# Attention's opening in a fused attention and mixture-of-experts kernel: what is computed while the decay mask is fetched, and the order of small work in the loop

## The chip, the core and the metric

The kernel runs on one core of a Trainium2 chip. Five engines have queues of their own: TensorE (PE), VectorE (DVE), ScalarE (ACT), GpSimd (POOL) and SyncE (SP). Each works through its queue in order. DMAs are issued from the queues of SP, ACT and POOL. The metric is the time on the device of one execution, in microseconds; smaller is better.

## The reference

Three layers follow each other: linear attention with a decay per head in blocks, a mixture of experts that routes each token to one expert, and a second mixture in which all experts contribute. The change lies in the first layer and the routing of the second.

```python
B, H, S, D = 2, 8, 768, 64          # batch, heads, sequence, head dimension
Dmask = where(rel >= 0, lam ** rel, 0)      # rel = i - j, one mask for each head
for b in range(nb):                         # blocks of the sequence
    intra = einsum('bhic,bhjc->bhij', qb, kb) * Dmask
    intra = einsum('bhij,bhjd->bhid', intra, vb)
    inter = einsum('bhid,bhde->bhie', qb * lam_pow, kv_state)
    out[:, :, sl] = intra + inter
    kb_dec = kb * rev_pow                   # rev_pow = lam ** (block - 1 - pos)
    kv_state = lam_block * kv_state + einsum('bhsd,bhse->bhde', kb_dec, vb)
# x: 1536 tokens of 512
logits = x @ w_gate + modality_bias[modality_id]
e_idx = argmax(logits);  gate_w = softmax(logits)[e_idx]
out[mask] = gate_w[mask, None] * (relu(x[mask] @ w1[e]) @ w2[e])     # 8 experts
# then the second mixture: gates balanced over rows and columns, all 8 experts summed
```

## The kernel before

The order on every engine is the order in which the code is written; nothing is rescheduled. Attention runs over M = 12 chunks of 128 tokens of one batch entry, all eight heads at once; chunk m is block m // 2 of batch entry m % 2. The function `attention_and_routing` holds all of it.

For each chunk, `load(m, 0)` and `load(m, 1)` bring the two halves of a packed input into one of four buffers `pk`: the first half holds keys and queries transposed, the second keys and values. `scores(m)` multiplies keys and queries into banks 0 and 1 of PSUM, `masked(m)` multiplies them by `maskT` on DVE, and so frees the banks. `scaled(m)` makes on POOL the decayed keys `kd` (with `revp`) and the scaled queries `qd` (with `lamq`). `outputs(m)` adds the products of `qd` with the state `St` and of values with the masked scores in bank 2, which ACT copies to `xT`; it also makes the new state from `kd` and the values in bank 3. `decay(m)` scales the state on POOL.

The mask isn't an input. DVE builds the powers of lambda in `pw`, one row a head, ACT's queue writes them to `powd` in device memory, and SP's queue reads them back in a shifted pattern as `maskT`, and as `lamq`. `revp` is a column of the mask.

The routing follows behind. `rows(m)` multiplies `xT` by an identity and the gate weights (`gtab`), so that one product gives the tokens' rows and their logits. `gates(m)` works on two chunks: it adds the modality's bias (prepared once by `setup`), finds the largest logit, the expert (`oh`), the sum of exponentials and its reciprocal `gw`, the gate weight. `weighted(m)` copies the rows with that weight and stores them to `xs`. `place(m)` counts positions within the experts, in bank 3. In step t of the loop stand `scores(t)`, `rows(t - 2)`, `outputs(t - 1)`; in odd steps also `gates(t - 3)` and the weighted copies, in even ones `place(t - 4)`. At t = 8 `early_table` picks the largest expert so far, whose weights are then loaded, and at t = 9 `ids_out` makes the row numbers of its first tokens.

## Time and profile before

| | |
|---|---|
| median of 3 timed runs | 1303.19 us (1300.23 to 1305.47) |
| profiled execution | 1302.41 us, of which the span of the trace is 1300.6 |
| PE, busy | 1256.5 us, 97% of the span |
| DVE, ACT, POOL, busy | 686.2 (53%), 499.5 (38%), 421.2 us (32%) |
| PE, first slice of 32.5 us of the span | 5 tenths |

The page gives the busy time of each engine and cuts the span in 40 slices. A line of the timeline gives the start, the time that the instructions took together, the engine, the line of the code, what is written and read, and in brackets how long the engine stood idle before it and what released it. An engine's name with a q is its queue, which issues DMAs. The granted clock is 1.00 at 2.4 GHz and 0.50 at 1.2 GHz.

### The profile page before, as it was taken

To read this page: it belongs to the slowest core of one execution; us is meant where nothing else is said; L and a number is where in the kernel's file an instruction comes from. 1 tells how busy PE (TensorE), PEld (TensorE's weight loads), DVE (VectorE), ACT (ScalarE), POOL (GpSimd) and SP (SyncE) were. 2 spreads that over 40 slices of the span, in tenths; PEclk is the share of its full clock that TensorE was granted. 3 is DMA by queue.
4 is the path that set the end of the run, shared out by engine and by line. 5 is a ranking of instruction groups with operands and counts; after the bars stand their busy time and mean duration, and the time that the engine had idled before them with its cause. 6 is when DMAs were issued, how large, how long until landed. Compare 5 with 4: busy or idle time off the path is not lost.

```text
span 1300.6 us, 19334 instructions
## 1 busy us (share of the span) xinstructions
PE 1256.5 (97%) x7266; PEld 1144.0 (88%) x7266; DVE 686.2 (53%) x1330; ACT 499.5 (38%) x996; POOL 421.2 (32%) x405
## 2 busy tenths in 40 slices
PE   5877999989999999999999999999999999999998
PEld 4867999988999999999999999999999999999997
DVE  5567787736354454545454546354535454545453
ACT  1244555531243334433434342234434343343431
POOL 3411101023333333333333336333333333333332
PEclk9988999989999999999999999999999999999999
DMA  8653565520122212221212223122222122222211
GB/s 284 204 180 115 198 197 188 163 98 1 41 65 66 74 57 74 65 65 65 74 65 74 72 74 100 58 77 66 65 74 65 66 65 65 66 73 65 69 38 49
DMA packets 60632, 117.76 MB, mean 91 GB/s; under 512 B 7288, under 2 KB 8960, under 8 KB 60528
## 3 DMA queue, kind: packets, MB, share of 16 engines
q1 hardware_dynamic: 55744, 105.67, 25.2%
q0 software_dynamic: 2304, 7.05, 1.6%
q10 hardware_dynamic: 2480, 3.71, 0.8%
q8 instruction: 59, 0.97, 0.3%
q14 instruction: 45, 0.37, 0.1%
HBM read 110.10 MB, written 6.30 MB: 89 GB/s over the span
## 4 chain that ended last, share of the span: by engine, by line
PE 78%; DVE 1%; POOL 0%; issue 0%; POOLq 0%
PE banks L887 13%; PE banks L886 13%; PE banks L885 13%; PE banks L850 12%; PE banks L851 12%; PE banks L852 12%; PE banks L723 0%; POOL out_dram L868 0%; PE banks L729 0%; PE banks L755 0%; DVE Pm L749 0%; DVE Pm L759 0%; DVE tab L747 0%; POOLq L1022 0%; DVE tab L757 0%
## 5 line engine op out<-in xcount | busy, mean ns | idle before, releaser
L839 POOL TENSOR_TENSOR w1r<-sraw,w1r 128x1024 fp32r<-128x1024 f32 x56 | 134.5, 2402 | 574.8 <-ACT w1r L838 574.8
L887 PE MATMUL banks<-w2r,hb 128*128 128x512 f32 x750 | 294.8, 393 | 0.0
L886 PE MATMUL banks<-w2r,hb 128*128 128x512 f32 x750 | 294.1, 392 | 0.0
L885 PE MATMUL banks<-w2r,hb 128*128 128x512 f32 x750 | 291.6, 389 | 0.0
L887 PEld LDWEIGHTS banks<-w2r,hb 128*128 128x128 f32 x750 | 140.7, 188 | 29.6
L855 ACT ACTIVATE hb<-snap 128x384 fp32r<-128x384 f32 x168 | 87.8, 523 | 200.7 <-DVE snap L972 120.0
L850 PE MATMUL banks<-x2T,w1r 128*128 128x384 f32 x464 | 159.3, 343 | 3.5 <-DVEq L702 3.5
L851 PE MATMUL banks<-x2T,w1r 128*128 128x384 f32 x464 | 158.9, 343 | 0.0
L852 PE MATMUL banks<-x2T,w1r 128*128 128x384 f32 x464 | 157.7, 340 | 0.0
L886 PEld LDWEIGHTS banks<-w2r,hb 128*128 128x128 f32 x750 | 140.7, 188 | 19.3
L885 PEld LDWEIGHTS banks<-w2r,hb 128*128 128x128 f32 x750 | 140.8, 188 | 19.1
L852 PE MATMUL banks<-xt,w1r 128*128 128x384 f32 x448 | 151.1, 337 | 0.0
L850 PE MATMUL banks<-xt,w1r 128*128 128x384 f32 x448 | 150.8, 337 | 0.0
L851 PE MATMUL banks<-xt,w1r 128*128 128x384 f32 x448 | 150.8, 337 | 0.0
L856 DVE SCALAR_TENSOR_TENSOR hb<-snap,hb 128x384 fp32r<-128x384 f32 x168 | 102.7, 611 | 66.4 <-ACT hb L855 66.4
L856 DVE SCALAR_TENSOR_TENSOR hb<-banks,hb 128x384 fp32r<-128x384 f32 x88 | 49.0, 557 | 165.0 <-ACT hb L855 165.0
L855 ACT ACTIVATE hb<-banks 128x384 fp32r<-128x384 f32 x88 | 43.3, 492 | 212.5 <-PE banks L852 204.9
L281 DVE TENSOR_TENSOR w2r<-stg,w2r 128x512 fp32r<-128x512 f32 x155 | 106.7, 691 | 3.7 <-ACT w2r L280 3.3
L280 ACT ACTIVATE w2r<-stg 128x512 fp32r<-128x512 f32 x155 | 96.2, 623 | 3.8 <-DMA stg<-in_w_dram 3.8
L850 PEld LDWEIGHTS banks<-x2T,w1r 128*128 128x128 f32 x464 | 88.1, 190 | 9.3 <-ACTq L702 3.7
L851 PEld LDWEIGHTS banks<-x2T,w1r 128*128 128x128 f32 x464 | 88.2, 190 | 5.7
L851 PEld LDWEIGHTS banks<-xt,w1r 128*128 128x128 f32 x448 | 84.1, 188 | 7.3
(218 smaller groups left out, 2114.4 us busy)
## 6 DMA issues: line engine op xcount, KB each, us to landing
stg<-in_w_dram SPq DMA_DIRECT2D x349, 256.0 KB
pk<-in_pack_dram SPq DMA_DIRECT2D x24, 512.0 KB
xs<-xr ACTq DMA_DIRECT2D x12, 256.0 KB
xrow<-in_w_dram SPq DMA_DIRECT2D x3, 256.0 KB
maskT<-powd SPq DMA_DIRECT2D x2, 256.0 KB
xrow<-xs,gidx POOLq DMA_INDIRECT x21
gtab<-in_gtab_dram ACTq DMA_DIRECT2D x1, 272.0 KB
lamq<-powd SPq DMA_DIRECT2D x2, 128.0 KB
```

What stands on the lines that cost most here:

```text
L280: A.activation(out=dst[:, 0], in_=src, func=AF.Copy)
L281: eng.tensor_tensor(out=dst[:, 1], in0=src, in1=dst[:, 0].bitcast(F32), op=ALU.subtract)
L839: G.tensor_tensor(out=ws[:, 1], in0=sraw, in1=ws[:, 0].bitcast(F32), op=ALU.subtract)
L850: T.matmul(out=b, lhsT=w(0, kk), rhs=x(0, kk), start=start and kk == 0, stop=False, skip_group_check=True)
L851: T.matmul(out=b, lhsT=w(0, kk), rhs=x(1, kk), start=False, stop=False, skip_group_check=True)
L852: T.matmul(out=b, lhsT=w(1, kk), rhs=x(0, kk), start=False, stop=stop and kk == kks - 1, skip_group_check=True)
L855: A.activation(out=h[:, 0], in_=src, func=AF.Relu)
L856: V.scalar_tensor_tensor(out=h[:, 1], in0=src, scalar=0.0, in1=h[:, 0].bitcast(F32), op0=ALU.max, op1=ALU.subtract)
L885: T.matmul(out=bank[mi], lhsT=h[:, 0, tok], rhs=w[:, 0], start=first, stop=False, skip_group_check=True)
L886: T.matmul(out=bank[mi], lhsT=h[:, 0, tok], rhs=w[:, 1], start=False, stop=False, skip_group_check=True)
L887: T.matmul(out=bank[mi], lhsT=h[:, 1, tok], rhs=w[:, 0], start=False, stop=last, skip_group_check=True)
```

## The change

Six things change.

- Both halves of chunk 1 are loaded ahead of the mask. The two loads of `lamq` are issued ahead of chunk 2, and `gtab` behind the other small loads of ACT's queue.
- `revp` no longer comes from the mask: a matmul with the constant `fold` copies the powers in `pw` to all partitions, and DVE copies them from bank 2.
- `outputs` is split; its state part is now `states(m, at)`. Scores of chunk 1 (in banks 6 and 7) and the states of chunks 0 and 1 (in banks 3 and 4) come ahead of the masking. So does `setup`. The loop begins at t = 2.
- In `gates` the sum and the reciprocal stand ahead of the choice of the expert. The store of the weighted rows is a function of its own, `stored`, issued behind the copy of `xT`.
- `place`, `early_table` and `ids_out` use columns of bank 3 from 256 on, beside the states.
- `ids_out` moves from the end of step t = 9 to a place ahead of `gates(6)` and `outputs(8)`.

```diff
         def place(m, ends=False):
             n = 3 if ends else 2
-            rv = bank[3][:, 0:n * NE].rearrange("p (m e) -> p m e", e=NE)
+            rv = bank[3][:, 256:256 + n * NE].rearrange("p (m e) -> p m e", e=NE)
...
         def early_table():
-            tot = bank[3][:, 32:40]
+            tot = bank[3][:, 288:296]
...
                 load(0, 0)
                 load(0, 1)
+                load(1, 0)
+                load(1, 1)
                 V.memset(pw[:, 0:127], 0.0)
...
                 A.dma_start(out=powd, in_=pw)
                 for h in range(2):
                     SP.dma_start(out=maskT[:, h], in_=bass.AP(tensor=powd.tensor, offset=powd.offset + 256 * h, ap=[[1, 128], [512, 4], [1, C]]))
-                load(1, 0)
-                load(1, 1)
-                A.dma_start(out=gtab, in_=i["gtab"])
                 A.dma_start(out=cst, in_=i["cst"])
...
                 A.dma_start(out=wg2f, in_=i["wg2"])
-                load(2, 0)
+                A.dma_start(out=gtab, in_=i["gtab"])
                 for h in range(2):
                     SP.dma_start(out=lamq[64 * h:64 * h + 64], in_=bass.AP(tensor=powd.tensor, offset=powd.offset + 256 * h + 128, ap=[[0, 64], [512, 4], [1, C]]))
+                load(2, 0)
                 load(2, 1)
...
+                def score_banks(m):
+                    return bank[6:8] if m == 1 else bank[0:2]
...
-                            T.matmul(out=bank[h][:, g * C:(g + 1) * C], lhsT=kT[r, g], rhs=qT[r, g], start=True, stop=True)
+                            T.matmul(out=score_banks(m)[h][:, g * C:(g + 1) * C], lhsT=kT[r, g], rhs=qT[r, g], start=True, stop=True)
...
                     A.activation(out=xT[m % 2], in_=o.rearrange("p (g i) -> p g i", g=4), func=AF.Copy)
+
+                def states(m, at=3):
+                    c, b = divmod(m, B)
+                    v = pk[m % 4][:, 1536:2048]
                     if c < NCH - 1:
-                        kv = bank[3][:, 0:256].rearrange("p (g e) -> p g e", g=4)
+                        kv = bank[at][:, 0:256].rearrange("p (g e) -> p g e", g=4)
...
                     V.tensor_tensor(out=eq, in0=lg, in1=bc(mx, 2, sh), op=ALU.is_equal)
+                    V.tensor_reduce(out=sx, in_=ex, axis=AX.X, op=ALU.add)
+                    V.tensor_scalar(out=sx, in0=sx, scalar1=1e-9, scalar2=None, op0=ALU.add)
+                    V.reciprocal(out=gw, in_=sx)
                     V.tensor_tensor(out=eq, in0=eq, in1=bc(k("w8"), 1, sh), op=ALU.mult)
                     V.tensor_reduce(out=mw, in_=eq, axis=AX.X, op=ALU.max)
                     V.tensor_tensor(out=oh[:, m:m + 2], in0=bc(k("w8"), 1, sh), in1=bc(mw, 2, sh), op=ALU.is_equal)
-                    V.tensor_reduce(out=sx, in_=ex, axis=AX.X, op=ALU.add)
-                    V.tensor_scalar(out=sx, in0=sx, scalar1=1e-9, scalar2=None, op0=ALU.add)
-                    V.reciprocal(out=gw, in_=sx)
...
-                    A.dma_start(out=xs[m * C:(m + 1) * C, :], in_=xw)
+
+                def stored(m):
+                    A.dma_start(out=xs[m * C:(m + 1) * C, :], in_=xr[m % 4])
 
                 scores(0)
-                V.tensor_copy(out=revp.rearrange("p (g h) -> p h g", h=2), in_=maskT[:, :, :, C - 1])
+                rp = bank[2][:, 0:H]
+                T.matmul(out=rp, lhsT=pw[:, 127:255], rhs=k("fold")[0:H], start=True, stop=True)
+                V.tensor_copy(out=revp, in_=rp)
+                scaled(0)
+                scaled(1)
+                scores(1)
+                setup()
+                states(0)
+                states(1, 4)
                 masked(0)
-                scaled(0)
-                for t in range(1, M + 1):
+                masked(1)
+                outputs(0)
+                load(4, 0)
+                load(4, 1)
+                for t in range(2, M + 1):
                     if t < M:
                         scores(t)
                         masked(t)
-                    if t == 2:
-                        setup()
-                    decay(t - 1)
+                    if t > 2:
+                        decay(t - 1)
...
-                    if t >= 2:
-                        rows(t - 2)
+                    rows(t - 2)
                     if t % 2 == 0 and t >= 4:
                         place(t - 4)
-                    if t % 2 and t >= 3:
+                    if t == MEARLY + 4:
+                        ids_out(gidx[1], MEARLY + 1, 3, bank[3][:, 296:302])
+                    if t % 2:
                         gates(t - 3)
                         weighted(t - 3)
                     outputs(t - 1)
-                    if t % 2 and t >= 3:
+                    if t > 2:
+                        states(t - 1)
+                    if t % 2:
+                        stored(t - 3)
                         weighted(t - 2)
+                        stored(t - 2)
...
                     if t == MEARLY + 4:
-                        ids_out(gidx[1], MEARLY + 1, 3, bank[3][:, 40:46])
                         gather_rows(1, (MEARLY + 1) * C)
...
                 weighted(M - 2)
                 weighted(M - 1)
+                stored(M - 2)
+                stored(M - 1)
```

On PE, from the first score matmul to the rows of chunk 1, before (pk_127 to pk_130 are the buffers of chunks 0 to 3; L441 scores, L472 outputs, L479 states, L489 rows):

```order
L441 MATMUL banks<-pk_127 128x128 x8
L441 MATMUL banks<-pk_128 128x128 x8
L472 MATMUL banks<-At_134,pk_127 64x128 x8
L479 MATMUL banks<-pk_127,kd_138 64x64 x8
L441 MATMUL banks<-pk_129 128x128 x8
L489 MATMUL banks<-gtab,xT_140 128x136 x4
L472 MATMUL banks<-At_135,pk_128 64x128 x8
L479 MATMUL banks<-pk_128,kd_139 64x64 x8
L441 MATMUL banks<-pk_130 128x128 x8
L489 MATMUL banks<-gtab,xT_141 128x136 x4
```

And in the change (L444 scores, L527 the fold matmul, L486 states, L475 outputs, L496 rows):

```order
L444 MATMUL banks<-pk_127 128x128 x8
L527 MATMUL banks<-cst,pw 128x8
L444 MATMUL banks<-pk_128 128x128 x8
L486 MATMUL banks<-pk_127,kd_138 64x64 x8
L486 MATMUL banks<-pk_128,kd_139 64x64 x8
L475 MATMUL banks<-At_134,pk_127 64x128 x8
L444 MATMUL banks<-pk_129 128x128 x8
L496 MATMUL banks<-gtab,xT_140 128x136 x4
L475 MATMUL banks<-At_135,pk_128 64x128 x8
L444 MATMUL banks<-pk_130 128x128 x8
L496 MATMUL banks<-gtab,xT_141 128x136 x4
```

The scores of chunk 1 and both groups of states moved ahead of the outputs of chunk 0; between those and the scores of chunk 2 nothing stands any more.

On DVE, from the decay of the keys to the masking of chunk 2, before (At_134 and At_135 are the masked scores of even and odd chunks; the casts of `trib` and `midf` and the lines to `wg2s` are `setup`):

```order
L517 COPY revp<-maskT 128x2x4
L445 TENSOR_TENSOR At_134<-banks,maskT 128x512 x2
L445 TENSOR_TENSOR At_135<-banks,maskT 128x512 x2
L483 COPY St_146<-banks 128x256
L445 TENSOR_TENSOR At_134<-banks,maskT 128x512 x2
L426 CAST trib<-cst 128x128
L427 CAST midf<-midr 128x12
L428 TENSOR_TENSOR btok<-midf,mb 128x96
L429 TENSOR_SCALAR midf<-midf 128x12
L430 TENSOR_TENSOR tmpb<-midf,mb 128x96
L431 TENSOR_TENSOR btok<-btok,tmpb 128x96
L433 TENSOR_TENSOR wg2s<-wg2f,wg2s 128x4x8
```

And in the change:

```order
L528 COPY revp<-banks 128x8
L426 CAST trib<-cst 128x128
L427 CAST midf<-midr 128x12
L428 TENSOR_TENSOR btok<-midf,mb 128x96
L429 TENSOR_SCALAR midf<-midf 128x12
L430 TENSOR_TENSOR tmpb<-midf,mb 128x96
L431 TENSOR_TENSOR btok<-btok,tmpb 128x96
L433 TENSOR_TENSOR wg2s<-wg2f,wg2s 128x4x8
L490 COPY St_146<-banks 128x256
L490 COPY St_147<-banks 128x256
L448 TENSOR_TENSOR At_134<-banks,maskT 128x512 x2
L448 TENSOR_TENSOR At_135<-banks,maskT 128x512 x2
```

`setup` and both copies of the states moved ahead of the first masking, which now has that of chunk 1 right behind it.

On ACT, the loop's step t = 3, before (L500 the exponential, L513 the weighted copies, L514 their store, L473 the copy to `xT`):

```order
L500 ACTIVATE sm_84<-sm_84 128x16
L513 ACTIVATE xr_142<-banks,sm_85 128x256 x2
L514 DMA xs<-xr_142 128x512
L473 ACTIVATE xT_140<-banks 128x512
L513 ACTIVATE xr_143<-banks,sm_85 128x256 x2
L514 DMA xs<-xr_143 128x512
L473 ACTIVATE xT_141<-banks 128x512
```

And in the change (L507, L520, L523 and L476):

```order
L507 ACTIVATE sm_84<-sm_84 128x16
L520 ACTIVATE xr_142<-banks,sm_85 128x256 x2
L476 ACTIVATE xT_140<-banks 128x512
L523 DMA xs<-xr_142 128x512
L520 ACTIVATE xr_143<-banks,sm_85 128x256 x2
L523 DMA xs<-xr_143 128x512
L476 ACTIVATE xT_141<-banks 128x512
```

The first store moved behind the copy to `xT`.

## Rows read from the trace of the kernel before

**Rows 1.** Busy time by stretch: us, engines' busy (instructions), granted clock, DMA share, GB/s.

```profile
0.00:14.40 14.40, 2.08 (x16) 1.79 (x16) 3.85 (x16) 1.28 (x1) 1.25 (x5) 1.00 0.73 250
...
33.70:38.90 5.20, 5.18 (x59) 4.75 (x59) 0.85 (x6) 0.99 (x3) 0.00 (x0) 0.67 0.26 93
```

**Rows 2.** Timeline of the opening: start us, us, engine, line, tiles, [idle before].

```profile
12.99 0.17 DVE L517 COPY revp<-maskT 128x8 f32<-128x8 f32 x1 [8.29 <-DMA maskT<-powd]
...
14.44 2.08 PE L441 MATMUL banks<-pk 64*128 64x128 f32 x16 [7.75 <-DVE At L445]
...
21.05 1.19 PE L489 MATMUL banks<-gtab,xT 128*128 128x136 f32 x8
...
23.10 0.63 PE L479 MATMUL banks<-pk,kd 128*64 128x64 f32 x16
...
23.66 1.16 PE L441 MATMUL banks<-pk 64*128 64x128 f32 x16
```

**Rows 3.** Timeline around `rows(2)`, loop step t = 4.

```profile
29.71 1.19 DVE L502 TENSOR_TENSOR sm<-sm,cst 128x16 f32<-128x16 f32 x1
...
31.82 0.84 ACT L513 ACTIVATE xr<-banks,sm 128x256 f32<-128x256 f32 x2 [2.84 <-DVE sm L507]
...
33.07 0.60 ACT L473 ACTIVATE xT<-banks 128x512 f32<-128x512 f32 x1 [0.41 <-ACT xr L513]
...
33.72 1.50 PE L489 MATMUL banks<-gtab,xT 128*128 128x136 f32 x8 [4.17 <-ACT xT L473]
...
35.21 1.97 PE L468 MATMUL banks<-qd,St 64*64 64x128 f32 x16
...
37.12 1.45 PE L472 MATMUL banks<-At,pk 128*64 128x128 f32 x16
```

**Rows 4.** Timeline around `rows(4)`, loop step t = 6.

```profile
43.10 0.16 DVE L505 TENSOR_REDUCE sm<-sm 128x2 f32<-128x16 f32 x1
...
43.69 0.84 ACT L513 ACTIVATE xr<-banks,sm 128x256 f32<-128x256 f32 x2 [0.97 <-DVE sm L507]
...
44.56 0.33 ACTq L514 DMA_DIRECT2D xs<-xr  x1
...
44.94 0.60 ACT L473 ACTIVATE xT<-banks 128x512 f32<-128x512 f32 x1 [0.40 <-PE banks L441]
...
45.59 1.19 PE L489 MATMUL banks<-gtab,xT 128*128 128x136 f32 x8 [0.74 <-ACT xT L473]
...
46.77 1.09 PE L468 MATMUL banks<-qd,St 64*64 64x128 f32 x16
...
47.79 1.09 PE L472 MATMUL banks<-At,pk 128*64 128x128 f32 x16
```

**Rows 5.** SP's queue in 2.0-5.5, 5.5-7.5, 7.5-12.5 us: packets, MB, share.

```profile
q1 hardware_dynamic: 280, 1.02, 75.7%
q1 hardware_dynamic: 16, 0.01, 1.4%
q1 hardware_dynamic: 1234, 1.26, 74.9%
```

**Rows 6.** SP's own waits; the issue of the lambda loads.

```profile
SPq L416 <- DMA mb<-in_mbias_dram: 2.2, 1, 2.2
...
11.22 1.47 SPq L416 DMA_DIRECT2D lamq<-powd  x2
```

**Rows 7.** Timeline: the activation table, a state's copy.

```profile
6.65 1.28 ACT L473 ACT_TABLE_LOAD   x1 [6.65 <-DMA pk<-in_pack_dram]
...
19.32 0.42 DVE L483 COPY St<-banks 128x256 f32<-128x256 f32 x1 [1.52 <-PE banks L479]
```

**Rows 8.** Timeline around `ids_out`, loop steps t = 8 to 10.

```profile
63.14 0.95 DVE L344 TENSOR_TENSOR idp<-cst,idt 128x768 bf16<-128x768 f32 x1
...
67.59 0.29 PE L349 MATMUL banks<-idr,idp 128*128 128x6 bf16 x6 [2.44 <-DVE St L481]
...
69.12 2.18 PE L489 MATMUL banks<-gtab,xT 128*128 128x136 f32 x8
```

More of the change, by code (lines that the diff above doesn't have):

```diff
@@ L440, in scores @@
                             r = slice(64 * h, 64 * h + 64)
-                            T.matmul(out=bank[h][:, g * C:(g + 1) * C], lhsT=kT[r, g], rhs=qT[r, g], start=True, stop=True)
+                            T.matmul(out=score_banks(m)[h][:, g * C:(g + 1) * C], lhsT=kT[r, g], rhs=qT[r, g], start=True, stop=True)
                 def masked(m):
                     for h in range(2):
-                        V.tensor_tensor(out=At[m % 2][:, h], in0=bank[h], in1=maskT[:, h].rearrange("p g i -> p (g i)"), op=ALU.mult)
+                        V.tensor_tensor(out=At[m % 2][:, h], in0=score_banks(m)[h], in1=maskT[:, h].rearrange("p g i -> p (g i)"), op=ALU.mult)
                 def decay(m):
```

## The prediction

> **What bounds the kernel now.** I read the page's line of busy shares first: TensorE (PE) is busy nearly throughout, so only a place where it stands still, or runs at its lower clock, can give time back. I then cut the span by stretches. The change lies in attention, so I looked where PE is idle before about 89 us. The opening is the largest such place: of the first 14.4 us PE works 2.08, the sixteen score matmuls of chunk 0 [rows 1]. In the order of time, VectorE (DVE) waits 8.29 us for the mask and copies `revp` at 12.99, and the scores of chunk 1 start at 14.44 because they need the banks that masking chunk 0 frees [rows 2]. Their sixteen matmuls take 2.08 us; the same ones at 23.66 take 1.16. TensorE ran at its lower level of 1.2 GHz from the restart until 21.05, where a `rows` group first shows the fast 1.19 us [rows 2], although the column of the granted clock shows 1.00 there.
>
> The second place is `rows(2)`, in loop step t = 4: PE waits 4.17 us for `xT` of chunk 2 [rows 3]. The reader is to follow ScalarE (ACT) backwards there: `xT` starts at 33.07 behind the two weighted copies of chunk 0 and their store, and these waited until 31.82 for the gate weight, the last of `gates(0)` on DVE. DVE came to those gates late, since `setup` stood in its queue before the masking of chunk 3, and it was slow in them: one small product took 1.19 us beside a GpSimd product [rows 3]. Work starts again at a granted clock that averages 0.67 over 33.7 to 38.9 [rows 1]. The same wait without lateness is short: 0.74 us in t = 6 [rows 4], and as much in t = 8. The third place is `ids_out` in t = 9, where PE waits 2.44 us, and the next `rows` group then takes 2.18 us [rows 8].
>
> **The change part by part, and its sum.** PE work is not removed; the fold matmul adds one small pair in idle time. The sum therefore counts what leaves the stretch after the mask, and the stalls.
>
> Opening. Scores of chunk 1 and both state products move ahead of the mask. Their warm cost is 1.16 + 2 x 0.63 = 2.42 us [rows 2]. I take the warm price, not the 2.08 of the slow scores, because the slow stretch after a restart lasts about as long as before whatever stands in it. Against that, masking may begin later. DVE now has `setup` and both state copies ahead of it. `setup` needs the last small load on ACT's queue. The nearest row is SP's wait for `mb`, over at 11.22 [rows 6]; with the gate table no longer ahead of the small loads I take 10.9 for the last of them. Behind it come the activation table, 1.28, now waiting for that load, two state copies of 0.42 [rows 7], and 0.4 as an estimate for two small operations of the kind that take about 0.2: 13.4 us, against 13.07 where masking began before (12.99 plus the copy's start-to-start). So the start is 0.3 later and the term is 2.42 - 0.3 = **2.1 us**. Lower bound 0, if mask and setup both come 2 us later; upper bound 5.0, if the earlier products leave the clock high (the 6.6 us from 14.44 to 21.05 ran at 2.08 / 1.16 = 1.8 times the warm price, so 2.9 of them come back).
>
> The mask itself: its issue waits for `powd` as before, but the two halves of chunk 1 now stand ahead of it in SP's queue. That queue moved 280 packets (1.02 MB, the two halves of chunk 0) in 2.0 to 5.5 us, then only 16 packets until 7.5, and only then the mask's and what follows, 1234 packets until 12.5 [rows 5]. So the two further halves fall largely into a hole of 2 us in that queue. At the rate of the first row they need 3.5 us, and pushing the mask by 0 to 1.5 us is what the rows allow; up to 0.4 of it is hidden under the setup chain. I take 0.3, inside the 13.4. The Trainium skill, DMA: Bandwidth & Descriptors, section Queues, rings and completion order, says that each engine takes descriptors in the order of its ring, which speaks against putting anything in front of the mask. By that rule alone, with no hole to fill, the mask would come the whole 3.5 us later and the opening term would be -1.0 instead of 2.1 (13.0 + 3.5 against 13.4).
>
> `setup` costs nothing later: it ran behind the masking of chunk 2 and is now covered by the wait for the mask; without that cover it costs its place before the masking, which is counted above. Loads of chunks 2 and 3 are now issued behind both lambda loads and wait for the small loads; chunk 2 is needed only after `outputs(0)`, at about 16.5, and SP can issue it from 11.2 on. A start as long as that hole and 1.75 for a half (3.5 for two) end at 15. I cost it at 0; at most 1 us.
>
> The stall of `rows(2)`. With `setup` gone, `gates(0)` follows the masking of chunk 3 at once, ahead of the GpSimd products that slowed it. The nearest undelayed case is t = 6 [rows 4], where the wait is 0.74 and not 4.17, and the next paragraph takes that away too. The full 4.17 goes. With no such idle stretch the clock need not fall: `rows` 1.50 against 1.19, the state product 1.97 against 1.09, the masked product 1.45 against 1.09 [rows 3, 4], together 1.55. Term: **5.7 us**; bounds 0 (another wait takes its place) and 5.7.
>
> The regular stall. In odd steps the sums and the reciprocal now come before the three operations that pick the expert. L505 stood at 43.10 behind them [rows 4] and can go up to 0.6 earlier, but must wait for the exponential; I take 0.3. The store's issue, 0.33 on ACT's queue, moves behind `xT` [rows 4]. Together 0.63 of the 0.74 wait, twice (before `rows(4)` and `rows(6)`): **1.3 us**; bounds 0.7 (the store alone) and 1.5. The pick of the expert ends up to 0.7 later, but the placement that reads it stands a step later, except after the loop, where PE waits for it anyway and the next work waits for ACT.
>
> `ids_out` now stands before `outputs(8)` in a part of bank 3 that the state products don't use. It no longer waits for DVE's state update behind the gates, but it still needs `idp`, written until 64.09 [rows 8], while PE now reaches it some 2 us earlier. So part of the 2.44 stays, as a wait of about 1.8. I give 0.6 for the wait (which also covers the expert total that no longer waits for a state update) and 0.6 of the 0.99 (2.18 - 1.19) lost at the lower clock: **1.2 us**; bounds -0.5 (a longer wait in front of `outputs(8)`) and 3.4.
>
> Last two gates (t = 11 and after the loop): there ACT and DVE lead, weighted copies, stores and weight splits stand in one queue whose sum stays, so only the earlier gate weight counts, twice 0.3: **0.6 us**; bounds 0 and 1.4.
>
> Sum: 2.1 + 5.7 + 1.3 + 1.2 + 0.6 = 10.9 us. The profiled execution took 1302.4 us (span 1300.6), which gives 1291.5. The median of the three timed runs is 0.8 above it; I put the prediction between, at 1292. What follows attention waits on loads that are issued relative to it, so I let the whole gain through.
>
> **Rivals.** (a) The mask comes late, with all 3.5 us of the two halves in front of it. For it speaks that the queue was full at 12.5; against it the hole from 5.5 to 7.5 [rows 5]. 3.1 us of the gain go: 1295. This is what the skill's rule on the ring's order would do here. (b) The stall in t = 4 is replaced by another. DVE masks four chunks in quick succession before `gates(0)`; or a load is late. For it: the small products of `gates(0)` take over 1 us when GpSimd works beside them [rows 3]. Then 5.7 us stay: 1298, no change that can be told. (c) The clock is up when the mask lands, since PE works from about 7 to 11 us: 2.9 more, 1289. (d) Slower: the queue of DVE. Everything from the first masking on stands behind the last small load, so each microsecond that it lands after 10.9 costs one. It decides from 10.9 + 10.9 = 21.8 us on, and past about 28 us the kernel is slower beyond the measurement, 1310. Against it: `mb` was in at 11.22 [rows 6] with the mask's packets in flight as they will be now. (e) The overlap doesn't happen: the fold matmul waits for the constants, the scores of chunk 1 stand behind it on PE, and if they come with the mask the 2.1 us are lost: 1294.
>
> **How the numbers follow.** Chances: forecast 0.58, (a) 0.14, (b) 0.12, (c) 0.08, (d) 0.04, (e) 0.04. The forecast's own spread, from the bounds of the two middling terms, is 1289.5 to 1295. The range 1288.5 to 1297.5 takes in (a), (c) and (e) and half of (b), with the 0.2% by which the timed runs of before spread. A change of 0.5%, 6.5 us, is about what a measurement of this kernel can tell. Faster beyond it: forecast, (a), (c), (e), 0.84; (b) gives 0.12 for the same; (d) 0.04.
>
> **What would show it.** In the changed profile: scores of chunk 1 and both state groups before 12 us, `outputs(0)` at 14.5 to 15; scores of chunk 4 at about 26 instead of 28.4; no wait over 1 us before `rows(2)` and no fall of the granted clock at 34; waits of 0.1 to 0.3 before `rows(4)` and `rows(6)`; a wait of 1.5 to 2 before `ids_out`. A masking that begins after 15 us, or a new wait in t = 3 or t = 4, makes the prediction wrong.

## The result, and the profile after

The changed kernel took 1288.31 us (median of 4 runs, 1287.42 to 1289.38) beside 1303.52 us of the kernel before (4 runs, 1300.23 to 1305.47): a ratio of 0.9895, 95% interval 0.9877 to 0.9912. Its profiled execution took 1288.1 us with a span of 1286.2, so 14.4 us of the span are gone where the sum had 10.9. The median is 3.7 us below the forecast and 0.2 below the lower end of its range.

The busy time by stretch answers to [rows 1]. The first stretch is the opening, the second the 5.2 us behind `rows(2)`, which now starts at 26.7. Columns as there.

```profile
0.00:14.40 14.40, 6.26 (x66) 5.61 (x66) 6.04 (x23) 1.51 (x2) 2.27 (x6) 1.00 0.80 243
...
26.70:31.90 5.20, 5.18 (x78) 4.78 (x79) 2.94 (x11) 1.33 (x3) 2.99 (x4) 1.00 0.85 295
```

In the opening PE works 6.26 us instead of 2.08. Behind `rows(2)` the granted clock is 1.00 where it was 0.67. The timeline of the opening answers to [rows 2]:

```profile
9.93 0.56 PE L527 MATMUL banks<-cst,pw 8*128 8x8 f32 x2 [3.21 <-DMA cst<-in_cst_dram]
10.42 2.08 PE L444 MATMUL banks<-pk 64*128 64x128 f32 x16
12.43 1.68 PE L486 MATMUL banks<-pk,kd 128*64 128x64 f32 x32
...
13.60 0.99 DVE L490 COPY St<-banks 128x256 f32<-128x256 f32 x2
14.51 2.47 DVE L448 TENSOR_TENSOR At<-banks,maskT 128x512 f32<-128x512 f32 x4
...
15.84 1.09 PE L475 MATMUL banks<-At,pk 128*64 128x128 f32 x14 [0.16 <-DVE At L448]
17.38 1.16 PE L444 MATMUL banks<-pk 64*128 64x128 f32 x16 [0.46 <-DMA pk<-in_pack_dram]
...
25.35 1.16 PE L444 MATMUL banks<-pk 64*128 64x128 f32 x16
```

The fold matmul (L527) waits 3.21 us for the constants. Behind it PE works off the scores of chunk 1 (L444 at 10.42) and both states (L486), until 14.1 and not before 12 as foretold. DVE copies the states (L490) and goes on to the masking without a wait, at 14.51 and not at 13.4; `outputs(0)` starts at 15.24 instead of 14.5 to 15. So it is PE's work behind the constants that masking waits for, not the mask. The scores of chunk 4 nevertheless start at 25.35, 3.04 earlier than before and earlier than the 26 foretold, since the outputs of chunk 0 (L475, 14 of 16 in 1.09) and the scores of chunk 2 run at the fast price at once. The scores of chunk 2 also wait 0.46 us for their load.

The store of `powd` on ACT's queue, and the mask's issue on SP's, which waits for it:

```profile
4.79 0.28 ACTq L406 DMA_DIRECT2D powd<-pw  x1
...
9.43 0.97 SPq L408 DMA_DIRECT2D maskT<-powd  x2
```

That step of the prediction was wrong. Before, the mask was issued at 5.50, now at 9.43, because `powd`, 8 KB issued on ACT's queue at 4.79, is written only then. No wait of DVE for the mask comes of it, as the rows above show. The queues' packets (q1 is SP's, q10 ACT's) answer to [rows 5], first 2.0 to 5.5 us, then 5.5 to 7.5:

```profile
q1 hardware_dynamic: 301, 1.10, 93.0%
q10 hardware_dynamic: 2, 0.00, 0.0%
...
q1 hardware_dynamic: 190, 0.72, 88.9%
```

While SP's queue moved its four half loads, ACT's moved 2 packets in the first stretch and none in the second (it has no row there). The Trainium skill, DMA: Bandwidth & Descriptors, section Queues, rings and completion order, says that a DMA engine takes turns between the rings that have work. By that rule `powd` would have come through between the loads; the trace does not show such turns here.

Around `rows(2)`, answering to [rows 3] and [rows 4], and PE's waits for `xT` from 20 to 66 us (us in total, times, longest):

```profile
25.62 1.02 DVE L514 TENSOR_TENSOR oh<-cst,sm 128x16 bf16<-128x16 f32 x1
...
26.72 1.19 PE L496 MATMUL banks<-gtab,xT 128*128 128x136 f32 x8 [0.21 <-ACT xT L476]
...
PE banks L496 <- ACT xT L476: 0.2, 1, 0.2
```

The 4.17 us are 0.21, the only such wait: `rows(4)`, `rows(6)` and `rows(8)` have none. One product of `gates(0)` still takes 1.02 us (L514), beside a GpSimd product that starts at 25.56, but it picks the expert and stands behind the gate weight now. Around `ids_out`, answering to [rows 8]:

```profile
53.98 0.30 PE L349 MATMUL banks<-idr,idp 128*128 128x6 bf16 x6 [1.51 <-DVE idp L344]
...
55.79 1.98 PE L475 MATMUL banks<-At,pk 128*64 128x128 f32 x16
```

It waits 1.51 us (1.8 was foretold), now for `idp` itself. Then the clock falls: from 55.79 to 57.70 the granted clock is 0.50, and `outputs(8)`, here 1.98 us, takes 1.09 elsewhere.

Last the end of attention, which the prediction showed no rows of. Before (L500 exponential, L513 weighted copies, L514 stores, L280 the first weight split, L489 `rows(10)`, L584 a matmul that waits for DVE):

```profile
87.93 0.21 ACT L500 ACTIVATE sm<-sm 128x16 f32<-128x16 f32 x1 [1.57 <-DVE sm L499]
89.11 0.84 ACT L513 ACTIVATE xr<-banks,sm 128x256 f32<-128x256 f32 x2 [0.97 <-DVE sm L507]
...
91.28 1.08 ACTq L514 DMA_DIRECT2D xs<-xr  x1
92.41 1.15 ACT L280 ACTIVATE w1r<-stg 128x512 fp32r<-128x512 f32 x2 [1.16 <-issue]
...
80.82 1.19 PE L489 MATMUL banks<-gtab,xT 128*128 128x136 f32 x8 [1.29 <-ACT xT L473]
...
101.06 0.60 PE L584 MATMUL banks<-hb,w2l 128*128 128x272 f32 x1 [4.68 <-DVE hb L312]
```

After (L507, L520, L523, L280, L496, L609):

```profile
75.94 0.22 ACT L507 ACTIVATE sm<-sm 128x16 f32<-128x16 f32 x1 [1.57 <-DVE sm L506]
76.79 1.20 ACT L520 ACTIVATE xr<-banks,sm 128x256 f32<-128x256 f32 x3 [0.64 <-DVE sm L511]
...
78.39 0.33 ACTq L523 DMA_DIRECT2D xs<-xr  x1
78.77 1.15 ACT L280 ACTIVATE w1r<-stg 128x512 fp32r<-128x512 f32 x2 [0.40 <-ACT xr L520]
...
68.80 1.19 PE L496 MATMUL banks<-gtab,xT 128*128 128x136 f32 x8
...
87.43 0.39 PE L609 MATMUL banks<-hb,w2l 128*128 128x272 f32 x1 [2.73 <-DVE hb L312]
```

From the exponential to the weight split ACT took 4.48 us and takes 2.83. DVE's queue behind that split is the same work as before (its hidden layer `hb` starts 8.16 and 8.17 us after the split), so PE gets `hb` earlier by as much. `rows(10)`, which waited 1.29 us, waits for nothing.

### The profile page after: what moved, and what is told of

It is laid out like the page before. It is cut to its first block, busy times and chain, and to the rows that moved or that the text cites. A ratio compares the mean times of both kernels' runs of the same rounds, so it can differ in the third digit from the quotient of the medians.

```text
span 1286.2 us, 19343 instructions
## 1 busy us (share of the span) xinstructions
PE 1253.0 (97%) x7268; PEld 1139.9 (89%) x7268; DVE 683.8 (53%) x1330; ACT 499.0 (39%) x996; POOL 421.3 (33%) x405
## 4 chain that ended last, share of the span: by engine, by line
PE 78%; DVE 1%; POOL 0%; issue 0%; POOLq 0%
PE banks L912 13%; PE banks L911 13%; PE banks L910 13%; PE banks L875 12%; PE banks L876 12%; PE banks L877 12%; PE banks L748 1%; POOL out_dram L893 0%; PE banks L754 0%; PE banks L780 0%; DVE Pm L774 0%; DVE Pm L784 0%; DVE tab L772 0%; POOLq L1047 0%; DVE tab L782 0%
## 5 line engine op out<-in xcount | busy, mean ns | idle before, releaser
L280 ACT ACTIVATE w2r<-stg 128x512 fp32r<-128x512 f32 x155 | 96.2, 623 | 4.3 <-DMA stg<-in_w_dram 4.3
```

Of the source, the lines that this page charges most:

```text
L280: A.activation(out=dst[:, 0], in_=src, func=AF.Copy)
```

## The experiments

All fourteen traces are read with one table. It cuts the time at five starts that every trace has: the scores of chunks 4, 5, 9 and 11, and the matmul that waits for `hb` behind the last gates (101.06 before, 87.43 after). Each entry is the difference of two starts, in us; the last is the rest of the span.

| kernel | scores(4) starts | 4 to 5: `rows(2)` | 5 to 9: regular stalls | 9 to 11: `ids_out` | 11 to `hb`: last gates | rest |
|---|---|---|---|---|---|---|
| before | 28.39 | 10.57 | 21.39 | 13.79 | 26.92 | 1199.54 |
| changed | 25.35 | 5.06 | 19.77 | 13.15 | 24.10 | 1198.77 |
| c1_changed_again | 26.26 | 4.78 | 19.78 | 12.00 | 24.09 | 1201.69 |
| e1_setup_only | 28.50 | 5.60 | 21.40 | 13.79 | 26.99 | 1202.82 |
| e2_gates_stores_only | 27.48 | 11.18 | 19.77 | 15.21 | 24.08 | 1198.88 |
| e3_opening_only | 26.94 | 11.08 | 21.41 | 13.79 | 27.72 | 1199.16 |
| e6_loads_only | 28.53 | 5.65 | 21.39 | 14.01 | 26.73 | 1200.59 |
| e5_setup_back | 26.21 | 8.17 | 19.78 | 11.99 | 24.09 | 1202.06 |
| e4_ids_back | 25.53 | 4.78 | 19.77 | 13.99 | 24.19 | 1199.54 |
| e10_ids_mid | 25.29 | 4.96 | 19.77 | 12.53 | 24.86 | 1199.69 |
| e9_stores_back | 24.87 | 5.61 | 20.79 | 12.51 | 25.14 | 1196.78 |
| e12_gates_back | 27.23 | 4.78 | 20.38 | 12.09 | 26.37 | 1198.85 |
| e7_small_first | 25.17 | 4.78 | 19.77 | 12.00 | 24.09 | 1197.79 |
| e13_small_first_ids_mid | 24.72 | 4.78 | 19.78 | 12.52 | 24.87 | 1197.33 |

The last column is work that no kernel here changes, and it differs by 6 us from trace to trace. Differences of 1 to 2 us between kernels are therefore read from the other columns.

**One part alone.** Only `setup` moved, in the kernel before:

```diff
+                setup()
                 masked(0)
...
-                    if t == 2:
-                        setup()
```

> The kernel before, with setup alone moved ahead of the first masking. Theory (the wait before rows(2) came from DVE being late by setup): masking of chunk 3 starts about 1.9 us earlier, gates(0) runs ahead of the GpSimd products, the wait of 4.2 us falls to about 1 and the granted clock stays up after it: 4 to 5.5 us faster than before. Rival (the wait comes from the order of sums and stores): the wait stays above 3 us, gain at most 1 us.

Measured: 1298.68 us (10 runs, 1296.93 to 1300.84), beside 1302.28 of before (31 runs); ratio 0.997 (0.9956 to 0.9984). DVE, POOL and PE around `rows(2)`:

```profile
27.41 0.17 DVE L502 TENSOR_TENSOR sm<-sm,cst 128x16 f32<-128x16 f32 x1
...
28.72 1.04 POOL L456 TENSOR_TENSOR kd<-pk,revp 128x512 f32<-128x512 f32 x1 [1.88 <-issue]
...
30.41 1.19 PE L489 MATMUL banks<-gtab,xT 128*128 128x136 f32 x8 [0.74 <-ACT xT L473]
```

The small product that took 1.19 us [rows 3] takes 0.17, since GpSimd, whose next product starts at 28.72, has been idle for 1.88 us then, and the stall is the regular 0.74. The median is 3.6 us lower, a little less than the 4 to 5.5 expected. In the trace 4.97 us of the stretch are gone, and no other column before the last moves by more than 0.11; the lead of 4.78 at `hb` shrinks to 1.5 in the rest of this execution.

Only the gate weight and the stores (the lines of the change in `gates`, `weighted`, `stored` and their calls):

```diff
+                    V.reciprocal(out=gw, in_=sx)
                     V.tensor_tensor(out=eq, in0=eq, in1=bc(k("w8"), 1, sh), op=ALU.mult)
...
                     outputs(t - 1)
                     if t % 2 and t >= 3:
+                        stored(t - 3)
                         weighted(t - 2)
+                        stored(t - 2)
```

> The kernel before, with only the sums ahead of the choice of the expert and the stores behind the copy of xT. Theory: waits before rows(4) and rows(6) fall from 0.74 to about 0.1, the wait before rows(2) from 4.2 to about 3.2 (clock still falls), and the end of attention, where both last stores now stand behind both weighted copies, gives 1.0 to 1.7: in all 3 to 5 us faster. Rival (this order alone removes the long wait): 8 us or more. Rival (the end of attention gives nothing): 2.3 us.

Measured: 1294.49 us (10 runs), ratio 0.9942 (0.9923 to 0.9962). The times spread widely, five from 1290.6 to 1293.7 and five from 1295.3 to 1299.0; the profiled execution (1298.43) is one of the slower:

```profile
29.01 0.98 DVE L499 TENSOR_TENSOR sm<-sm,sm 128x16 f32<-128x16 f32 x1
...
32.26 2.18 PE L489 MATMUL banks<-gtab,xT 128*128 128x136 f32 x8 [3.04 <-ACT xT L473]
```

Here the stall is still there, with a slow product of 0.98 us ahead of it. The regular stalls (1.62 us) and 2.84 us at the last gates are gone: these two edits alone make both terms whole. The 7.8 us of the median are more than these 4.5. That the faster half misses the stall would explain it, but is not shown: no trace of a faster execution was taken.

Only the opening, with `setup` left in t = 2 (the change's loads, fold matmul, scores and states, the rest as before):

> The opening alone (loads, fold matmul, scores and states of two chunks ahead of the mask), with setup in step t = 2, gates, stores, ids_out and bank columns as before. Theory: scores of chunk 4 come 2.5 to 3.5 us earlier as in the changed kernel, but the wait before rows(2) stays at 3.5 us or more, since gates(0) is late: 2 to 4 us faster. Rival (the opening itself removes the wait): scores of chunk 5 come 8 us earlier, 8 us faster.

Measured: 1301.23 us (10 runs), ratio 0.9991 (0.9978 to 1.0004). Scores of chunk 4 start 1.45 earlier, not 2.5 to 3.5; the stall stays at 4.17, as the theory had it, and its stretch takes 11.08. The 2 to 4 us expected did not come: the interval includes no change. Only the order of the loads:

> The kernel before with only the order of the DMA issues changed (chunk 1 ahead of the mask, lambda loads ahead of chunk 2, gate table last). Theory after the result: the small transfers of ACT's queue wait behind four half loads, powd lands near 9.4 and the mask is issued there instead of at 5.5, masking starts 0.5 to 1.5 us later: 0.5 to 1.5 us slower. Rival (the prediction's step: two halves fill a hole, mask issued at 5.5): masking within 0.3 us of before, no change in time.

Measured: 1302.8 us (10 runs), ratio 1.0 (0.9983 to 1.0018). The profiled execution was one of three at 1296.3 to 1298.7; the other seven took 1301.3 to 1305.0. The mask's issue is late here too (8.13 instead of 5.50), and in this order DVE does wait for the mask: masking begins at 13.69, 0.62 later than before, within the theory's bounds.

```profile
23.55 0.26 DVE L430 TENSOR_TENSOR tmpb<-midf,mb 128x96 f32<-128x96 f32 x1
...
30.49 1.19 PE L489 MATMUL banks<-gtab,xT 128*128 128x136 f32 x8 [0.79 <-ACT xT L473]
```

`setup` stands where it did, but its product L430 (1.03 us beside GpSimd before) took 0.26, and the stall is 0.79. So whether the 4.17 us appear goes with which small operations of DVE meet a GpSimd product, and it can turn out well with `setup` in its old place. The two groups of times suggest that it differs from one execution to the next; the slower group has no trace.

**The changed kernel with one part put back.** `setup` again in t = 2:

```diff
-                setup()
                 states(0)
...
+                    if t == 2:
+                        setup()
```

> The changed kernel with setup back in step t = 2. Theory: what made the stall before rows(2) is that DVE's small operations of setup and gates(0) run beside GpSimd's products (1.0 to 1.3 us instead of 0.17); with setup back DVE comes to gates(0) later and meets them again: a wait of 2 to 4 us before rows(2), a granted clock under 0.8 over the 5 us behind it, in all 4 to 6 us slower than the changed kernel, 1292 to 1294, or two groups of times about 5 us apart if the meeting is by chance. Rival: the earlier gate weight and the later stores alone keep the wait under 0.5, and setup's place is worth no more than its own length: 0 to 1 us slower, 1288 to 1289.

Measured: 1292.94 us (6 runs, 1292.48 to 1295.54), ratio 0.9936 (0.9918 to 0.9955). DVE, POOL and PE, and the 5.3 us behind `rows(2)` by stretch:

```profile
27.61 1.11 DVE L512 TENSOR_TENSOR sm<-sm,cst 128x16 f32<-128x16 f32 x1
...
27.43 1.27 POOL L461 TENSOR_TENSOR qd<-pk,lamq 128x512 f32<-128x512 f32 x1
...
29.11 1.90 PE L496 MATMUL banks<-gtab,xT 128*128 128x136 f32 x8 [1.73 <-ACT xT L476]
...
29.10:34.40 5.30, 5.29 (x61) 4.80 (x61) 2.41 (x10) 1.08 (x3) 0.62 (x1) 0.68 0.57 213
```

The theory holds, with a wait a little under the 2 to 4 us expected: the product that takes 1.11 us runs beside GpSimd's, the wait is 1.73 and the clock averages 0.68 behind it, together 3.4 us more than in c1. The stretch is shorter than before (8.17 against 10.57); that the earlier weight and the later stores do this is not shown, since e2 has both and takes 11.18. The Trainium skill, SBUF — State Buffer, section Who interferes with whom, says that a DVE instruction with two inputs in SBUF contends with a GpSimd one that reads it, and that reductions do not contend; that agrees with the traces, where the products of `gates(0)` take up to 1.19 us and its reductions never over 0.17.

`ids_out` again at the end of t = 9, still in columns 296 to 302:

```diff
-                    if t == MEARLY + 4:
-                        ids_out(gidx[1], MEARLY + 1, 3, bank[3][:, 296:302])
...
                     if t == MEARLY + 4:
+                        ids_out(gidx[1], MEARLY + 1, 3, bank[3][:, 296:302])
                         gather_rows(1, (MEARLY + 1) * C)
```

> The changed kernel with ids_out at the end of step t = 9, where it stood before, but still in its new part of bank 3. Theory: in the changed kernel TensorE stands 1.51 us before ids_out (idp is written until 53.9), and the three groups behind it then run at the lower clock and lose 0.55 + 0.89 + 0.22 = 1.66 us. At the end of the step outputs(8) and states(8) come first, idp is there, no bank is shared with a state update: wait 0 to 0.3, no fall of the clock, so 2.5 to 3.2 us faster than the changed kernel, 1285 to 1286. Rival A: the new place is itself the gain, and the old one brings the wait of 2.44 us back: 0.5 to 1 slower, 1289. Rival B: DVE is behind here and another wait of 1 to 1.5 us takes the place, at scores(10) for the banks: within 0.7 of the changed kernel.

Measured: 1291.42 us (4 runs, 1289.6 to 1291.87), ratio 0.9923 (0.9895 to 0.9952).

```profile
57.47 0.29 PE L349 MATMUL banks<-idr,idp 128*128 128x6 bf16 x6 [2.59 <-DVE St L488]
```

The theory fell, rival A came: 2.59 us, for the state's update on DVE, although the columns are no longer shared. So other columns of the same bank do not remove the wait; another bank was not tried. The median is 3.1 us above the first one of the changed kernel, more than the rival's 0.5 to 1. Between `outputs(8)` and `states(8)`:

```diff
                     outputs(t - 1)
+                    if t == MEARLY + 4:
+                        ids_out(gidx[1], MEARLY + 1, 3, bank[3][:, 296:302])
                     if t > 2:
                         states(t - 1)
```

> The changed kernel with ids_out between outputs(8) and states(8). Theory: ids_out costs a wait because TensorE reaches it before idp (written until 53.9) and, at the end of the step, because the states that stand ahead of it in the same bank must first be read by DVE. Behind decay(8) and outputs(8), about 54.3, idp is there and no state product of the step stands ahead: wait 0 to 0.2 before ids_out, at most 0.8 before states(8), which then waits for the read of the ids in the same bank, no fall of the clock. Step t = 9 takes 5.3 to 6 us instead of 8.15 and the kernel is 2 to 3 us faster than the changed one. Rival: the wait only moves, states(8) waits 1.5 us or more for DVE behind its masking, the clock falls behind it: within 0.7 us.

Measured: 1289.43 us (4 runs, 1287.85 to 1290.82), ratio 0.9901 (0.9879 to 0.9922).

```profile
56.95 0.15 DVE L350 TENSOR_REDUCE idf<-banks 128x3 f32<-128x6 f32 x1
...
57.16 0.69 PE L486 MATMUL banks<-pk,kd 128*64 128x64 f32 x16 [2.57 <-DVE idf L350]
```

The wait only moved, as the rival had it: `states(8)` writes the same bank and waits 2.57 us until DVE, with `gates(6)` ahead in its queue, has read the ids (L350). No fall of the clock follows here (L486 takes 0.69). By the times the two places are not told apart (1289.43 and 1288.0 in c1, ranges overlapping); by the table the place in the change is 0.5 us better than this one in the `ids_out` column and 0.8 in the next, taken from c1; in the first trace of the changed kernel the `ids_out` column is 0.6 us worse.

All stores again right behind their copies (`stored` empty, the issue back in `weighted`), and the gate weight again last in `gates`:

> The changed kernel with every store again right behind its weighted copies; the earlier gate weight stays. The prediction shared the 0.63 us of the regular stall as 0.33 for the store's issue and 0.3 for the gate weight. Theory: by these shares waits of 0.3 to 0.45 us come back before rows(4), rows(6) and rows(8), about 1 us in all, and with the issues in the tail (1.08 against 0.33 us on ACT's queue) 1.5 to 3 us slower than the changed kernel, 1290 to 1291. Rival A: the gate weight alone removes the regular stall (waits under 0.15) and the tail keeps its gain: within 0.7 us. Rival B: the store's issue is the whole of it: waits of 0.6 to 0.75 before each, and the tail as before, 3.5 us slower.

> The changed kernel with the gate weight again behind the three operations that pick the expert; the stores stay behind xT. Putting the stores back gave waits of 0.43 and 0.44 us before rows(4) and rows(6), so the store's part of the regular stall is about 0.4 and the gate weight's the other 0.3. Theory: with 0.3 us less lead, waits of 0.1 to 0.4 before rows(4) and rows(6), each weighted copy of the last two gates 0.33 later (the gap from the exponential to the copy 0.97 instead of 0.64), in all 1 to 2 us slower. Rival A: the stores alone have made enough room (the waits stay under 0.05): only the tail's 0.3 to 0.7. Rival B: the weight is also what keeps rows(2) from its stall: a wait over 1 us there and 4 us slower.

Measured: stores back 1290.22 us (4 runs, 1287.45 to 1291.51), ratio 0.9916 (0.9887 to 0.9945); weight back 1291.81 us (4 runs, 1289.52 to 1293.86), ratio 0.9918 (0.9894 to 0.9942). `rows` of chunks 2 and 4 with the stores back:

```profile
26.79 1.19 PE L496 MATMUL banks<-gtab,xT 128*128 128x136 f32 x8 [0.76 <-ACT xT L476]
...
36.80 1.19 PE L496 MATMUL banks<-gtab,xT 128*128 128x136 f32 x8 [0.43 <-ACT xT L476]
```

`rows` of chunk 4, and the last store's issue, with the weight back:

```profile
38.12 1.19 PE L496 MATMUL banks<-gtab,xT 128*128 128x136 f32 x8 [0.23 <-ACT xT L476]
...
80.23 1.91 ACTq L523 DMA_DIRECT2D xs<-xr  x1
```

In the column of the regular stalls the stores are worth 1.02 us and the weight 0.61, together 1.63, as much as the kernel before and the changed one differ by (1.62). The waits of 0.43 and 0.23 us are those that the two theories gave. At the last gates the stores are worth 1.04. With the weight back these cost 2.28 more, of which 1.58 is the issue of the last store, 1.91 us instead of 0.33 (below); in the median the weight costs 3.8 us beside c1, more than the 1 to 2 expected.

**The opening again.** Small loads ahead of `powd`, chunk 1 on ACT's queue:

```diff
                 A.dma_start(out=pw[:, 128:129], in_=i["lam"])
+                A.dma_start(out=cst, in_=i["cst"])
...
-                load(1, 0)
-                load(1, 1)
...
                 A.dma_start(out=powd, in_=pw)
+                for part in range(2):
+                    A.dma_start(out=pk[1][:, part * 1024:(part + 1) * 1024], in_=i["pack"][1, part])
```

> The changed kernel with the four small loads on ACT's queue ahead of powd's store, and chunk 1's halves on ACT's queue behind that store instead of on SP's ahead of the mask. Theory: the mask's issue, at 9.4 in the changed kernel, goes to 5 to 7, and masking chunk 0, at 14.5, begins 1 to 4 us earlier; but the scores of chunk 2 still wait for their load, since what the queues have to move up to there is the same, so they start at 16.5 to 17.5 (now 17.38) and the time is within 1 us of the changed kernel. Rival A: the late mask is what is left to win in the opening: scores of chunk 2 at 14 to 15.5 and 2 to 3 us faster. Rival B: chunk 1 comes so late from ACT's queue that masking chunk 1 waits for its scores: 1 to 3 us slower.

Measured: 1285.73 us (4 runs, 1283.34 to 1287.61), ratio 0.9878 (0.9846 to 0.991).

```profile
3.93 0.31 ACTq L408 DMA_DIRECT2D powd<-pw  x1
...
7.86 0.94 SPq L412 DMA_DIRECT2D maskT<-powd  x2
...
9.12 2.08 PE L444 MATMUL banks<-pk 64*128 64x128 f32 x16 [1.86 <-DMA pk<-in_pack_dram]
...
13.49 2.47 DVE L448 TENSOR_TENSOR At<-banks,maskT 128x512 f32<-128x512 f32 x4
...
16.73 1.64 PE L444 MATMUL banks<-pk 64*128 64x128 f32 x16
```

`powd` still takes 3.9 us from its issue, now behind ACT's own small loads, so the mask's issue misses the 5 to 7 expected. Masking begins 1.02 us earlier, because the scores of chunk 1, which now wait for their own load, start at 9.12 instead of 10.42. The scores of chunk 2 start 0.65 earlier, within the theory's bounds; but they wait for no load, only for the outputs, which run at the slow price, so that the loads bind there was not shown. Together with the other place of `ids_out`:

> Both: the small loads ahead of powd's store with chunk 1 on ACT's queue, and ids_out between outputs(8) and states(8). If the two gains are at different places they add up: opening 0 to 1, ids_out 2 to 3, so 2 to 4 us faster than the changed kernel, 1284 to 1286 where that takes 1288. Rival: what follows attention gives back a lead by the level at which the clock stands after the last gates' stall (24.5 or 26 to 27 us from there to the next load split): under 1.5 us.

Measured: 1286.03 us (4 runs, 1285.81 to 1288.78), ratio 0.9881 (0.9859 to 0.9902). The gains do not add up, since e10 has none. And the changed kernel once more beside them:

> The changed kernel once more, beside the other three, to have its own time on the same chip and a second trace of it. Theory: nothing before rows(4) is by chance but the level of the clock when masking begins: 1287 to 1289.5, the wait before rows(2) under 0.5, the one before ids_out 1.5 again. Rival: the missing stall before rows(2) is by chance too, and one execution in some shows it: single times of 1291 or more.

Measured: 1288.0 us (4 runs, 1284.58 to 1290.38), ratio 0.988 (0.9857 to 0.9903). The copy of the second state on DVE, then PE at the outputs of chunk 0, the scores of chunk 2, and `ids_out`:

```profile
14.08 0.42 DVE L490 COPY St<-banks 128x256 f32<-128x256 f32 x1 [0.43 <-PE banks L486]
...
15.16 2.57 PE L475 MATMUL banks<-At,pk 128*64 128x128 f32 x16 [1.13 <-DVE At L448]
17.66 1.80 PE L444 MATMUL banks<-pk 64*128 64x128 f32 x16
...
54.62 0.30 PE L349 MATMUL banks<-idr,idp 128*128 128x6 bf16 x6 [1.52 <-DVE idp L344]
```

No stall before `rows(2)`. Masking starts at 14.42, right behind the copy that waited for the states on PE. The outputs of chunk 0 take 2.57 us here, not the fast price, although the granted clock reads 1.00, and `ids_out` waits 1.52 with no fall of the clock behind it. Both differ from the first trace. The kernels e7 and e13 lie some 2 us below this one, with ranges that overlap; they are not told apart from it.

## Why the prediction was right, and where its terms were off

The direction holds, and so do the mechanisms of the stalls, which are most of the sum; the path of the opening was wrong, and one term much too small. The sum was 3.5 us short of the first trace and 1.1 short of c1's 12.0. More than half of the 3.5 is the last gates' term. By the terms, first trace and c1:

- **Opening, 2.1: measured 3.04 and 2.13.** Where the number is near, it is by luck: two errors offset each other. The sum let masking begin behind the last small load, the activation table and the copies of the states, 13.4, and put the scores of chunk 1 and the states, PE's work "before 12 us", at nothing on that path. The runs show that this work is the path: fold matmul behind the constants, scores of chunk 1, states, copy of the second state, masking, 1.1 us later than foretold (c1: 1.0). In the ten traces with this opening masking starts 4.06 to 4.38 us after the scores of chunk 1 do, with `setup` there (c1: 4.37) or without (e3: 4.37, e5: 4.38). The mask's issue came 3.9 us later (c1: 2.6), against "its issue waits for `powd` as before", but DVE had no wait for the mask in any of them. So rival (a) had a lateness that did not bind, and the wait for the constants of rival (e), 3.21 us, is what moved masking, though the scores and states still came ahead of it. On the other side the warm price was too low for what moved: the slow stretch behind the masking lasted 6.6 us before and some 4 in c1 (from 15.16; the scores at 17.66, 1.80 us, lie between the prices), and in the first trace it is missing, which is rival (c). So the reason given, that the slow stretch lasts about as long as before whatever stands in it, did not hold. That PE was at 1.2 GHz there is read from prices alone: the granted clock reads 1.00 through all of these stretches.
- **Stall of `rows(2)`, 5.7: measured 5.51 and 5.79.** Right, also in the cause: e1 removes it by moving `setup` alone, e5 brings a shorter one back. What the prediction did not see is that the meeting of the products can turn out otherwise with `setup` in its old place (e6). That it does so now and then in the kernel before (1298.01 in one of 31 runs) is a guess; only one trace of it was taken.
- **Regular stalls, 1.3: measured 1.62 and 1.61.** The store counted more than its issue of 0.33, 0.51 a time by e9; the weight 0.30 by e12, as taken.
- **`ids_out`, 1.2: measured 0.64 and 1.79.** The wait was as foretold within 0.3; whether the clock falls behind it makes the difference. The reason given was half wrong: not the other columns but the place ahead of the states removes the wait for DVE (e4).
- **Last two gates, 0.6: measured 2.82 and 2.83.** This is the mis-sized term. It held that copies, stores and weight splits "stand in one queue whose sum stays". The sum of the queue stays, but not what stands ahead of `xT` and of the first split: 1.2 us of the wait of `rows(10)`, 0.33 of the weight, 0.46 between the two copies, and 0.75 in the issue of the last store.
- **The rest passed through:** 0.77 more and 2.15 less. The mean of that column over the thirteen other traces is 1199.5, before has 1199.54: the lead passes through, with up to 3 us either way.

## What to carry to other kernels

Where PE waits for a copy, list what stands ahead of that copy in its engine's queue, DMA issues included, at every place where it waits, the end of a stage too: the same two edits paid 1.6 us in the loop and 2.8 behind it. A stall made by small operations of DVE that meet GpSimd products is a matter of a microsecond's shift, so look at single times and a second trace before giving its length to one edit. And when big loads are put ahead on one queue, price the small transfers of the other queue that something waits for, and follow which of them binds: here the constants held masking up, not the mask.

## What the runs showed of the hardware

- An 8 KB store on ACT's queue took 1.6 us from issue to the release of SP before (3.90 to 5.50), and 4.2 to 5.8 us in the kernels with four half loads of 512 KB ahead on SP's queue.
- The issue of the same store on ACT's queue took 0.33 us in ten of fourteen traces, 0.99 to 1.09 in three and 1.91 in one. All four have the late gate weight; a fifth kernel with it has 0.33. What it waits for was not found.
- From the stall for `hb` to the next weight split's wait in PE the same work took 24.5 us in five traces and 26.0 to 27.2 in nine. In the 4 us from 88 on the granted clock was 1.00 in e9 and 0.59 in the changed kernel. Nothing in the code differs there.
- The granted clock does not tell the price of matmuls in the opening: before, it reads 1.00 from 14.44 to 21.05, where sixteen score matmuls take 2.08 us, and also at 23.66, where they take 1.16. At `ids_out` of the changed kernel it reads 0.50 where sixteen outputs take 1.98 us instead of 1.09.
